# Order of transfers in one issue queue: earlier loads, earlier x transposes, hash halves apart, first casts on another engine

## Chip, cores, metric

The kernel runs on one core of a Trainium2 chip. The metric is the device time of one execution in microseconds (us). PE is the matmul engine, DVE the vector engine, ACT the scalar engine, POOL GpSimd. SP is the engine that issues most DMA transfers (161 of 180 in the trace of before): one queue, q1 of the profile, and its timeline shows them one after another in program order.

## The reference

Attention with hashed buckets, then a feed-forward layer. Inputs q, k, v are (4, 8, 768, 64): 32 heads of 768 tokens.

```
q_bits = (q @ proj > 0); k_bits = (k @ proj > 0)          # 6 bits each
mask   = bucket(q_bits) == bucket(k_bits)
attn   = softmax(where(mask, q @ k.T / 8, -1e9));  x = attn @ v
h = x @ w_in;  out = (h * cos(h)) @ w_out                 # 512 -> 2048 -> 512
```

## The kernel before

It works head by head. A *slot* is one head's turn and has nine *units*; in each unit PE makes 512 columns of scores, ACT takes their exponential, and PE multiplies the previous head's exponentials with v. In between stand small jobs, hung into a table `plan[(slot, unit)]`, so a job's place in the program is one pair of numbers:

- `load_pair(m)`: q, k, v of heads 2m and 2m+1, 1.18 MB in three transfers.
- `transpose` (PE) and `cast`: q and k of a head into the layout for the scores.
- the hash: PE multiplies with `proj` (one half for q, one for k), DVE compares with zero, and `place_bits` copies the bits by DMA into the rows beside the head's q and k. Heads are hashed in groups. Without its bits a head's scores can't start.
- `to_features(b, t)`: a DMA transpose of 128 tokens of batch b's attention output, six for a batch. The feed-forward layer ("MLP") of the batch needs them; the first MLP stands before slot 11.

All these transfers go through SP (w_in and w_out go through POOL), and SP waits at each transfer for what it depends on (in the trace of before up to 4.9 us at an x transpose, for DVE's `xtok`).

```python
def load_pair(m, heads=2):                       # three nc.sync.dma_start, buffer shared with pair m-3
    ...
def place_bits(heads, bits):
    for j, hd in enumerate(heads):
        for r in range(2):
            a = 32 * j + r * NBITS
            nc.sync.dma_start(out=e_all[D:KEXT, hd % NE, :, r * HB:(r + 1) * HB],
                              in_=bits[a:a + NBITS])
def to_features(b, t):
    nc.sync.dma_start_transpose(out=xT[:, :, b * S + t * P:b * S + (t + 1) * P],
                                in_=xtok[b][:, t, :])
# ... cut ...
def hash_at(slot, u, heads):
    # ... cut: first() and second() hash one half each; second() ends with place_bits ...
    at(slot, u, first)
    at(slot, u + 1, second)
TRANSPOSE = {2: (0, 0), 3: (0, 4), 4: (1, 4), 5: (2, 0), ...}        # cut
HASH = {(1, 0): [2, 3], (2, 6): [4, 5], (4, 5): [6, 7], (6, 6): [8, 9, 10, 11]}
# ... cut ...
for hd in range(12, NH, GH):
    hash_at(hd - 2, 5, list(range(hd, hd + GH)))
for m in range(3, NH // 2):
    at(max(0, 2 * m - 7), {3: 1, 4: 8}.get(m, 2), load_pair, m)
for b in range(B - 1):
    for t, (d, u) in enumerate(((1, 0), (1, 2), (1, 5), (1, 8), (2, 3), (2, 6))):
        at(H * (b + 1) + d, u, to_features, b, t)
# ... cut: in the prologue, head 0 is cast by DVE and ACT, head 1 is hashed ...
```

The softmax here doesn't subtract the row's maximum and nothing guards it: scores larger than these inputs give would overflow.

Of the kernel before, what the change touches and what calls it, by code (L numbers as in the profile page):

```python
# [10 lines left out]
BF16 = mybir.dt.bfloat16  # L11
# [11 lines left out]
def kernel(  # L23
# [19 lines left out]
    P = 128  # L43
# [5 lines left out]
    GH = 4  # L49
    VW = D + 1  # L50
    UNIT = 512
    HB = SB // 2 * P
    NU = SB * S // UNIT
# [8 lines left out]
    p_bits = ctx.enter_context(tc.tile_pool(name="p_bits", bufs=2))  # L62
# [14 lines left out]
    def load_pair(m, heads=2):  # L77
        b, h = divmod(2 * m, H)
        t = p_nat.tile([P, 2, 3, SB * D], FP32, name="nat")
        for i in range(0, 2, heads):  # L80
            for w, x in enumerate((q, k, v)):
                nc.sync.dma_start(
                    out=t[:, i:i + heads, w],
                    in_=x[b, h + i:h + i + heads].rearrange("h (p t) d -> p h (t d)", t=SB),
                )
            nat[2 * m + i] = t[:, i]
            nat[2 * m + i + heads - 1] = t[:, i + heads - 1]
# [48 lines left out]
    def cast(hd, r, engine="dve"):  # L136
        out_ap = e_all[0:D, hd % NE, :, r * HB:(r + 1) * HB]
        in_ap = f32[hd][r * D:(r + 1) * D]
        if engine == "act":
            nc.scalar.mul(out=out_ap, in_=in_ap, mul=QK_PRESCALE)  # L140
        else:
            nc.vector.tensor_scalar(
                out=out_ap, in0=in_ap, scalar1=QK_PRESCALE, scalar2=None, op0=ALU.mult,
            )

    def threshold(dst, src):
        nc.vector.tensor_scalar(  # L147
            out=dst, in0=src, scalar1=0.0, scalar2=0.5, op0=ALU.is_gt, op1=ALU.subtract,
        )


    def hash_group(heads, w, bits, pool=None, name="tp"):
        jp = (pool or ps_t).tile([P, 512], FP32, name=name, space=PSUM)
        for j, hd in enumerate(heads):
            nc.tensor.matmul(  # L155
                out=jp[32 * j:32 * (j + 1), 0:HB],
                lhsT=projx,
                rhs=f32[hd][:, w],
                start=True,
                stop=True,  # L160
            )
        n = 32 * len(heads)
        threshold(bits[0:n, w], jp[0:n, 0:HB])
# [5 lines that stand above are left out]
                nc.sync.dma_start(  # L169
                    out=e_all[D:KEXT, hd % NE, :, r * HB:(r + 1) * HB],  # L170
                    in_=bits[a:a + NBITS],
                )


    def hash_direct(hd, w):
        jp = ps_t.tile([P, 512], FP32, name="tp", space=PSUM)
        for r in range(2):
            nc.tensor.matmul(
                out=jp[32 * r:32 * r + NBITS, 0:HB],
                lhsT=projx[:, r * NBITS:(r + 1) * NBITS],  # L180
                rhs=f32[hd][:, w],
                start=True,
                stop=True,
            )
        for r in range(2):
            threshold(
                e_all[D:KEXT, hd % NE, w, r * HB:(r + 1) * HB],
                jp[32 * r:32 * r + NBITS, 0:HB],
            )
# [148 lines left out]
    for start, b in MLP_AT.items():  # L338
        for t in range(SB if b < B - 2 else SB - BRIDGE):
            f0 = 0  # L340
            for i, n in enumerate(RATE):
                slot, u = divmod(start * NU + t * len(RATE) + i, NU)
# [10 lines left out]
    def at(slot, u, f, *args):  # L353
        plan.setdefault((slot, u), []).append((f, args))


    def hash_at(slot, u, heads):
        bits = []
        first_bank = (ps_y, "y") if slot < min(MLP_AT) else (ps_t, "tp")

        def first():
            bits.append(p_bits.tile([P, 2, HB], BF16, name="bits"))
            hash_group(heads, 0, bits[0], *first_bank)

        def second():
            hash_group(heads, 1, bits[0])
            place_bits(heads, bits[0])

        at(slot, u, first)
        at(slot, u + 1, second)  # L370

    def both(slot, u, f, hd, step=1):
        at(slot, u, f, hd, 0)
        at(slot, u + step, f, hd, 1)


    TRANSPOSE = {2: (0, 0), 3: (0, 4), 4: (1, 4), 5: (2, 0), 6: (3, 0), 7: (3, 4),
                 8: (4, 2), 9: (5, 0), 10: (5, 4), 11: (6, 0), 12: (7, 0)}
    CAST = {1: (0, 2), 2: (0, 6), 3: (1, 2), 4: (2, 3), 5: (3, 2), 6: (4, 0), 7: (5, 2),
            8: (6, 3), 9: (7, 2), 10: (7, 5)}  # L380
    HASH = {(1, 0): [2, 3], (2, 6): [4, 5], (4, 5): [6, 7], (6, 6): [8, 9, 10, 11]}
    for hd in range(2, NH):
        slot, u = TRANSPOSE.get(hd, (hd - 5, 0))
        both(slot, u, transpose, hd, 2 if hd < 12 else 3)
    for hd in range(1, NH):
        both(*CAST.get(hd, (hd - 3, 1)), cast, hd)
    for (slot, u), heads in HASH.items():
        hash_at(slot, u, heads)
    for hd in range(12, NH, GH):
        hash_at(hd - 2, 5, list(range(hd, hd + GH)))  # L390
    for hd in range(2, NH):
        at(max(0, hd - 3) if hd != 3 else 1, 4 if hd != 4 else 7, cast_v, hd)
    for m in range(3, NH // 2):
        at(max(0, 2 * m - 7), {3: 1, 4: 8}.get(m, 2), load_pair, m)

    for b in range(B - 1):
        for t, (d, u) in enumerate(((1, 0), (1, 2), (1, 5), (1, 8), (2, 3), (2, 6))):
            at(H * (b + 1) + d, u, to_features, b, t)

    with tc.manual_schedule():  # L400
        warm = glob.tile([P, 1], BF16, name="warm")
        nc.vector.memset(warm, 0.0)
        nc.vector.memset(projx, 0.0)
        load_pair(0, 1)
        nc.scalar.dma_start(out=projx[0:D, 0:NBITS], in_=proj)
        nc.scalar.dma_start(out=projx[D:2 * D, NBITS:2 * NBITS], in_=proj)
        make_identity(nc, ident)
        once = glob.tile([P, 1], FP32, name="once")
        nc.scalar.activation(out=once, in_=warm, func=ACTF.Exp)
        load_pair(1)  # L410
        load_pair(2)
        nc.vector.memset(v_all[:, :, :, D:VW], 1.0)
        nc.vector.memset(delta, DELTA)
        for i in range(NE):
            (nc.vector if i < 3 else nc.gpsimd).memset(e_all[D:P, i], 0.0)
        wp = ps_y.tile([P, 512], FP32, name="y", space=PSUM)
        for _ in range(6):
            nc.tensor.matmul(  # L418
                out=wp[0:1], lhsT=warm, rhs=warm.to_broadcast([P, 512]), start=True, stop=True
            )  # L420
        transpose(0, 0, "act")
        transpose(0, 1)
        cast(0, 0)
        cast(0, 1, "act")
        hash_direct(0, 0)
        hash_direct(0, 1)
        transpose(1, 0, "act", ps_o, "o_att")
        transpose(1, 1, "act", ps_o, "o_att")
        bits = p_bits.tile([P, 2, HB], BF16, name="bits")
        for w in range(2):  # L430
            hash_group([1], w, bits)
        place_bits([1], bits)
        cast_v(0)
        cast_v(1)

        for hd in range(NH + 1):
            for i in WEIGHTS.get(hd, ()):
                load_weight(i)
            if hd in MLP_AT:
                for c in range(2):  # L440
                    hidden(MLP_AT[hd], c, wide)
            for u in range(NU):
                if hd < NH:
                    scores(hd, u)
                if hd > 0:
                    attend(hd - 1, u * NA, (u + 1) * NA)
                for b, t, f0, f1 in fill.get((hd, u), ()):
                    project(b, t, f0, f1)
                for f, args in plan.get((hd, u), ()):
                    f(*args)  # L450
                for b, t, f0, f1 in fill.get((hd, u), ()):
                    if f1 == NFF:
                        emit_out(b, t, "act")
            if hd > 0:
                normalize(hd - 1)
                if hd == NH:
                    for t in range(SB):
                        to_features(B - 1, t)

        ys = [(ps_y, "y"), (ps_t, "tp"), (ps_t, "tp")]  # L460
        for t in range(SB - BRIDGE, SB):
            project(B - 2, t, 0, NFF, *ys[t % 3])
            emit_out(B - 2, t, "act")
        for c in range(2):
            hidden(B - 1, c, wide)
        for t in range(SB):
            project(B - 1, t, 0, NFF, *ys[t % 3])
            emit_out(B - 1, t, "act", 2 if t == SB - 1 else 1)
# [30 lines left out]
```

## Time and profile before

| | before |
|---|---|
| time, median of the first 3 runs | 337.91 us (337.78 to 338.3) |
| span of the profiled run | 336.0 us |
| PE busy | 321.0 us, 96% |
| PE's waits for DMA, 10 to 100 us | xT 5.5, nat 2.5, bits 0.2 us |

The profiled run took 337.76 us.

From the page of the kernel before: each engine's busy time, and the granted PE clock in 40 slices of 8.4 us (tenths of full speed, 9 is 90% or more).

```profile
PE 321.0 (96%) x2794; PEld 193.5 (58%) x2794; DVE 177.9 (53%) x364; ACT 242.4 (72%) x453; POOL 83.2 (25%) x219
...
PEclk9999999799599999999999999999999999999999
```

Two slices have a low clock, the eighth (59 to 67 us) and the eleventh (84 to 92 us). The list of PE's waits between 10 and 100 us (line that waited, releaser, us in total, times, longest; `nat` is what `load_pair` fills, `ext` holds the operands of the scores with their bits, `xT` is what `to_features` fills):

```profile
PE st L284 <- DMA xT<-xtok: 5.5, 1, 5.5
PE tp L123 <- DMA nat<-in_q_dram: 2.5, 1, 2.5
...
PE st L201 <- DMA ext<-bits: 0.2, 1, 0.2
```

Two waits count: a transpose waiting for q of a later head, and the MLP waiting for a DMA transpose. The timeline of SP says why these came late (start, duration, what was issued, how many):

```profile
47.56 6.18 SPq L169 DMA_DIRECT2D ext<-bits  x8
53.86 0.37 SPq L82 DMA_DIRECT2D nat<-in_q_dram  x1
54.28 0.46 SPq L82 DMA_DIRECT2D nat<-in_k_dram  x1
54.78 0.47 SPq L82 DMA_DIRECT2D nat<-in_v_dram  x1
...
70.25 6.76 SPq L169 DMA_DIRECT2D ext<-bits  x8
77.06 1.23 SPq L253 DMA_TRANSPOSE xT<-xtok  x1
```

The eight bit transfers from 47.56 us are those of heads 8 to 11, 0.77 us each. Pair 7's load, the three lines from 53.86, stands behind them. The eight from 70.25 us are those of heads 12 to 15; the sixth x transpose, issued at 77.06, stands behind those. The table by stretches (length, PE busy, other engines, granted clock, DMA share, GB/s) shows what follows. The DMA share is the time of the packets that start in the stretch over that of 16 engines, so it can exceed 1.

```profile
core 0: us, PE busy (x) PEld busy (x) DVE busy (x) ACT busy (x) POOL busy (x), PEclk, DMA share, GB/s
56.80:59.30 2.50, 0.02 (x1) 0.00 (x0) 0.20 (x2) 0.77 (x2) 1.91 (x5) 1.00 1.00 320
60.20:63.50 3.30, 3.30 (x26) 2.27 (x24) 2.13 (x4) 2.46 (x5) 2.05 (x5) 0.50 1.28 153
...
80.80:86.30 5.50, 0.00 (x0) 0.03 (x1) 1.01 (x3) 0.49 (x1) 4.56 (x12) 0.79 1.27 185
86.30:90.90 4.60, 4.60 (x15) 2.22 (x16) 1.16 (x3) 1.47 (x3) 0.52 (x3) 0.51 1.16 270
90.90:98.80 7.90, 7.90 (x51) 4.74 (x49) 6.55 (x12) 5.73 (x12) 0.00 (x0) 1.00 0.28 62
```

In 56.8-59.3 and 80.8-86.3 PE does nothing. After each there is a stretch at half clock, 0.50 and 0.51; then full clock again. So in this trace each wait is paid twice. From 91 us on PE is busy to the end: there is nothing to gain there.

### The profile page before, as it was taken

How to read it: one execution, taken by the hardware profiler on the slowest of the kernel's cores; microseconds unless marked ns; L12 is line 12 of the kernel's file. 1: busy time of each engine (PE TensorE's matmuls, PEld its weight loads, DVE VectorE, ACT ScalarE, POOL GpSimd, SP SyncE). 2: the span in 40 equal slices, each digit the busy share in tenths (PEclk: the TensorE clock that was granted, in tenths of full speed). 3: DMA queues.
4: the chain of work that ended last, by engine and by line, in shares of the span. 5: the costliest groups of instructions: out<-in, count | busy, mean ns of one | idle time of the engine just before them, and what ended most of it. 6: DMA issues, size and time to landing. Idle time of an engine off the chain costs nothing.

```text
span 336.0 us, 7162 instructions
## 1 busy us (share of the span) xinstructions
PE 321.0 (96%) x2794; PEld 193.5 (58%) x2794; DVE 177.9 (53%) x364; ACT 242.4 (72%) x453; POOL 83.2 (25%) x219
## 2 busy tenths in 40 slices
PE   7999997996799999999999999999999999999995
PEld 3467665753366656665666656665665666565442
DVE  6878776556284445445884434444884011198100
ACT  4689888785279867878779867888779896477211
POOL 9974557316302223322002222422000000000000
PEclk9999999799599999999999999999999999999999
DMA  7856666939900400690600500650300011510021
GB/s 233 299 150 171 154 168 131 269 60 154 246 11 33 154 22 26 205 235 7 188 5 0 174 33 8 206 111 5 53 1 2 31 59 38 109 50 1 33 94 62
DMA packets 34398, 33.55 MB, mean 100 GB/s; under 512 B 15060, under 2 KB 30396, under 8 KB 34364
## 3 DMA queue, kind: packets, MB, share of 16 engines
q1 hardware_dynamic: 30732, 28.76, 30.0%
q0 software_dynamic: 3328, 4.20, 8.6%
q8 instruction: 22, 0.36, 0.5%
q10 hardware_dynamic: 304, 0.13, 0.1%
q14 instruction: 12, 0.10, 0.1%
HBM read 27.27 MB, written 6.29 MB: 100 GB/s over the span
## 4 chain that ended last, share of the span: by engine, by line
PE 88%; DMA 5%; ACT 3%; DVE 2%; SPq 1%; issue 0%; ACTq 0%; DVEq 0%
PE y L310 18%; PE st L201 17%; PE st L284 14%; PE o_att L230 10%; PE o_att L284 10%; PE tp L310 6%; PE tp L123 6%; PE tp L155 3%; DMA xT<-xtok 3%; ACT pt L209 2%; DMA nat<-in_q_dram 2%; PE o_att L220 1%; PE y L155 1%; DMA ext<-bits 1%; PE y L418 1%; DVE ext L147 1%
## 5 line engine op out<-in xcount | busy, mean ns | idle before, releaser
L209 ACT ACTIVATE pt<-st 128x512 f16<-128x512 f32 x288 | 157.1, 607 | 36.9 <-PE st L201 34.2
L201 PE MATMUL st<-ext 128*128 128x512 bf16 (+1 forms) x384 | 107.7, 328 | 0.9 <-ACT pt L209 0.5
L230 PEld LDWEIGHTS <-pt 128*128 128x128 f16 x1152 | 71.9, 98 | 37.0 <-issue 1.8
L310 PE MATMUL y<-wout,gt 128*128 128x512 f16 x288 | 88.1, 378 | 0.0
L230 PE MATMUL o_att<-v_ext,pt 128*128 128x65 f16 x1152 | 82.5, 195 | 0.0
L201 PEld LDWEIGHTS <-ext 128*128 128x128 bf16 x384 | 36.3, 98 | 25.3 <-issue 12.8
L107 POOL CAST v_ext<-nat 128x192 f16<-128x192 f32 x64 | 22.6, 383 | 114.0 <-PE o_att L230 113.9
L292 ACT ACTIVATE cs<-st 128x384 f16<-128x384 f32 x76 | 37.1, 490 | 17.0 <-PE st L284 16.7
L296 DVE TENSOR_TENSOR gt<-st,cs 128x384 f16<-128x384 f32 x76 | 41.9, 556 | 12.8 <-ACT cs L292 7.5
L310 PEld LDWEIGHTS <-gt 128*128 128x128 f16 x384 | 31.1, 98 | 14.9
L296 DVE TENSOR_TENSOR gt<-o_att,cs 128x384 f16<-128x384 f32 x52 | 28.9, 556 | 17.5 <-ACT cs L292 14.3
L244 DVE RECIPROCAL rec<-o_att 128x6 f32<-128x6 f32 x32 | 6.2, 194 | 55.8 <-PE o_att L230 55.7
L123 PE MATMUL tp<-ident,nat 128*128 128x128 f32 x186 | 32.1, 284 | 2.5 <-DMA nat<-in_q_dram 2.5
L292 ACT ACTIVATE cs<-o_att 128x384 f16<-128x384 f32 x52 | 25.5, 491 | 7.1 <-PE o_att L284 7.0
L284 PE MATMUL st<-xT,win_100 128*128 128x384 f16 x76 | 25.3, 333 | 5.5 <-DMA xT<-xtok 5.5
L123 PEld LDWEIGHTS tp<-ident,nat 128*128 128x128 f32 x186 | 22.9, 145 | 9.3 <-issue 3.8
L284 PE MATMUL st<-xT,win_101 128*128 128x384 f16 x76 | 25.4, 334 | 0.0
L284 PE MATMUL st<-xT,win_102 128*128 128x384 f16 x76 | 25.2, 332 | 0.0
L284 PE MATMUL st<-xT,win_103 128*128 128x384 f16 x76 | 25.2, 331 | 0.0
L310 PE MATMUL tp<-wout,gt 128*128 128x512 f16 x96 | 21.2, 379 | 0.0
L284 PEld LDWEIGHTS <-win_100 128*128 128x128 f16 x128 | 12.7, 99 | 14.2 <-issue 6.4
L111 POOL TENSOR_TENSOR vacc<-nat 128x192 f32<-128x192 f32 x32 | 19.5, 609 | 0.0
(207 smaller groups left out, 365.4 us busy)
## 6 DMA issues: line engine op xcount, KB each, us to landing
out_dram<-o_sb SPq DMA_DIRECT2D x23, 256.0 KB
nat<-in_q_dram SPq DMA_DIRECT2D x15, 384.0 KB
nat<-in_k_dram SPq DMA_DIRECT2D x15, 384.0 KB
nat<-in_v_dram SPq DMA_DIRECT2D x15, 384.0 KB
wout<-in_moe_w_out_dram POOLq DMA_DIRECT2D x8, 256.0 KB, 8.5
ext<-bits SPq DMA_DIRECT2D x62, 9.0 KB
win_100<-in_moe_w_in_dram POOLq DMA_DIRECT2D x2, 256.0 KB, 5.3
win_101<-in_moe_w_in_dram POOLq DMA_DIRECT2D x2, 256.0 KB, 5.1
```

The source lines that it names most:

```text
L107: nc.gpsimd.tensor_copy(out=dst[:, r], in_=src[:, r])
L111: nc.gpsimd.tensor_add(acc, x[:, 0:3 * D], x[:, 3 * D:6 * D])
L123: nc.tensor.matmul(out=tp[:, i * P:(i + 1) * P], lhsT=nat[hd][:, w, i * 2 * D:(i + 1) * 2 * D], rhs=ident, is_transpose=True, start=(i == ...
L155: nc.tensor.matmul(out=jp[32 * j:32 * (j + 1), 0:HB], lhsT=projx, rhs=f32[hd][:, w], start=True, stop=True,)
L201: nc.tensor.matmul(out=st[:, o:o + n], lhsT=e[:, 1, jt * P:(jt + 1) * P], rhs=e[:, 0, c:c + n], start=True, stop=True,)
L209: nc.scalar.activation(out=pts[hd][:, u * UNIT:(u + 1) * UNIT], in_=st, func=ACTF.Exp, bias=EXP_BIAS, scale=EXP_SCALE,)
L230: nc.tensor.matmul(out=o_ps[:, qt * VW:(qt + 1) * VW], lhsT=pts[hd][:, jt * S + qt * P:jt * S + (qt + 1) * P], rhs=v_all[:, hd % NV, jt], ...
L244: nc.vector.reciprocal(out=rec, in_=o_ps[:, :, D:VW])
L284: nc.tensor.matmul(out=hp[:, 0:TOK], lhsT=win_t[ft][:, ff * P:(ff + 1) * P], rhs=xT[:, ft, b * S + c * TOK:b * S + (c + 1) * TOK], start=( ...
L292: nc.scalar.activation(out=cs, in_=hp[:, 0:TOK], func=ACTF.Sin, bias=math.pi / 2.0, scale=1.0)
L296: nc.vector.tensor_tensor(out=gt, in0=hp[:, 0:TOK], in1=cs, op=ALU.mult)
L310: nc.tensor.matmul(out=y_state[b, t], lhsT=gates[b, c][ff][:, tt * P:(tt + 1) * P], rhs=wout_t[:, ff], start=(ff == 0), stop=(ff == NFF - 1),)
```

## The change

Its intent: loads one slot sooner and in front of the bit transfers, x transposes in front of the next bits, hash halves apart, first casts on ACT.

```diff
-    def hash_at(slot, u, heads):
+    def hash_at(slot, u, heads, step):
...
-        at(slot, u + 1, second)
+        at(slot, u + step, second)
...
-    TRANSPOSE = {2: (0, 0), 3: (0, 4), 4: (1, 4), 5: (2, 0), ...
+    TRANSPOSE = {2: (0, 0), 3: (0, 4), 4: (1, 3), 5: (1, 8), ...
-    HASH = {(1, 0): [2, 3], (2, 6): [4, 5], (4, 5): [6, 7], (6, 6): [8, 9, 10, 11]}
+    HASH = {(0, 0, 1): [1], (1, 0, 1): [2, 3], (2, 3, 2): [4, 5], (4, 4, 2): [6, 7],
+            (6, 5, 3): [8, 9, 10, 11]}
...
-        hash_at(hd - 2, 5, list(range(hd, hd + GH)))
+        hash_at(hd - 2, 5, list(range(hd, hd + GH)), 3)
...
-        at(max(0, 2 * m - 7), {3: 1, 4: 8}.get(m, 2), load_pair, m)
+        at(*{3: (0, 1), 4: (1, 5)}.get(m, (2 * m - 8, 5)), load_pair, m)
...
-        for t, (d, u) in enumerate(((1, 0), (1, 2), (1, 5), (1, 8), (2, 3), (2, 6))):
+        for t, (d, u) in enumerate(((1, 0), (1, 2), (1, 4), (1, 7), (2, 0), (2, 3))):
...
-        cast(0, 0)
         cast(0, 1, "act")
+        cast(0, 0, "act")
...
-        bits = p_bits.tile([P, 2, HB], BF16, name="bits")
-        for w in range(2):
-            hash_group([1], w, bits)
-        place_bits([1], bits)
```

(Cut: one cast moved by one unit, and the transposes of a head written out so that their second half may fall into the next slot.)

More of the change, by code (lines that the diff above doesn't have):

```diff
@@ L374, in both @@
         at(slot, u + step, f, hd, 1)
-    TRANSPOSE = {2: (0, 0), 3: (0, 4), 4: (1, 4), 5: (2, 0), 6: (3, 0), 7: (3, 4),
+    TRANSPOSE = {2: (0, 0), 3: (0, 4), 4: (1, 3), 5: (1, 8), 6: (3, 0), 7: (3, 4),
                  8: (4, 2), 9: (5, 0), 10: (5, 4), 11: (6, 0), 12: (7, 0)}
-    CAST = {1: (0, 2), 2: (0, 6), 3: (1, 2), 4: (2, 3), 5: (3, 2), 6: (4, 0), 7: (5, 2),
+    CAST = {1: (0, 2), 2: (0, 6), 3: (1, 2), 4: (2, 4), 5: (3, 2), 6: (4, 0), 7: (5, 2),
             8: (6, 3), 9: (7, 2), 10: (7, 5)}
-    HASH = {(1, 0): [2, 3], (2, 6): [4, 5], (4, 5): [6, 7], (6, 6): [8, 9, 10, 11]}
+    HASH = {(0, 0, 1): [1], (1, 0, 1): [2, 3], (2, 3, 2): [4, 5], (4, 4, 2): [6, 7],
+            (6, 5, 3): [8, 9, 10, 11]}
     for hd in range(2, NH):
         slot, u = TRANSPOSE.get(hd, (hd - 5, 0))
-        both(slot, u, transpose, hd, 2 if hd < 12 else 3)
+        at(slot, u, transpose, hd, 0)
+        at(*divmod(slot * NU + u + (2 if hd < 12 else 3), NU), transpose, hd, 1)
     for hd in range(1, NH):
         both(*CAST.get(hd, (hd - 3, 1)), cast, hd)
-    for (slot, u), heads in HASH.items():
-        hash_at(slot, u, heads)
+    for (slot, u, step), heads in HASH.items():
+        hash_at(slot, u, heads, step)
     for hd in range(12, NH, GH):
-        hash_at(hd - 2, 5, list(range(hd, hd + GH)))
+        hash_at(hd - 2, 5, list(range(hd, hd + GH)), 3)
     for hd in range(2, NH):
```

## The prediction

> **What bounds it.** PE is busy 321.0 of 336.0 us (profile, part 1), and after 91 us no PE wait is listed: only the first 91 us can give anything. There PE waits 5.5 us for xT<-xtok and 2.5 us for nat<-in_q_dram (list of waits). After each the granted clock falls: 0.66 in 60-65 us, 0.50 in 85-90 us (table by stretches).
>
> **Why.** SP issues transfers in program order, one hash-bit transfer every 0.77 us (timeline of SP).
> - Eight run from 47.56 to 53.7 us; the load of q/k/v pair 7 stands behind them, issued at 53.86, though its place is in slot 7, near 48. Head 14's transpose needs it in slot 9: PE stands until 59.34.
> - Eight more run from 70.25 to 77.0 us; the sixth x transpose stands behind them, issued at 77.06, among the w_out loads. The first MLP's second half needs it: PE stands from about 80.8 to 86.3 us.
>
> **Gains.**
> 1. Pair loads move six units forward, pair 7's ahead of the bits of heads 8-11. Its buffer is free once GpSimd has summed head 9 (44.5 us), so it is issued near 45 and lands near 51. Gone: 2.5 us, plus 1.2 us of slow clock (slot 9 took 8.3 us; without the wait 5.8; a warm slot 4.6).
> 2. All x transposes go out by slot 10 unit 3, ahead of the next bits. Gone: 5.5 us, plus 2.4 us of slow clock (16 matmuls from 86.30 to 91.28, against 2.6 us warm; chain of waits).
>
> [...]
>
> **Prologue.** A 1.28 us cast leaves DVE for ScalarE (0.84 us); head 1's hash leaves the prologue. First scores near 8.3 instead of 10.26 us. But head 1's bits go out near 11.7 instead of 10.94 us and packets follow 1.4-1.6 us later; slot 1 starts near 14.9 instead of 14.33. I expect 0 to 0.6 us lost.
>
> **Hash halves apart.** PE's work is the same (0.77 us per half); at most 0.3 us gained.
>
> **Costs.** Bits of heads 6-11 now stand behind 1.18 MB loads, which took 4.2 to 6.4 us. Head 8's would land near 52, when slot 8 starts; its wait was 0.2 us and may become 0.4-0.8. [...] pair 8's packets (issued 58.43) began at 62.3, after those of the transpose issued at 57.01. The x transposes likewise stand behind pair 8's load; I expect three by 66.5, MLP start near 67.
>
> **Sum.** -3.7 - 7.9 + 0.4 (prologue) + 0.5 (bits) - 0.1 = -10.8 us: 337.9 becomes 327.1, 3.2% faster. Range 325.0 to 331.2. Faster by over 2%: 0.88; within 2%: 0.11; slower: 0.01.
>
> **What would show it.** Right: no PE wait for nat or xT over 0.5 us; no slow-clock stretch after 10 us; first MLP matmul near 67 us; that MLP 20.9 us long; everything after parallel to before. Prologue: first scores near 8.3, slot 1 no earlier than before.
>
> **What would make it wrong.** Bits behind loads stop PE over 1 us at slots 6 or 8; w_out loads come late; x transposes behind pair 8's load delay the MLP's start; head 1's bits come early enough for the prologue to give its 2 us.

The sum: its 1.2 and 2.4 us of slow clock are read from the trace of before (at 86.30 us four matmuls took 1.44 us, against 0.65 at full clock). That trace has the packets of the transpose issued at 57.01 us from 59.76 to 63.57, and those of pair 8's load, issued at 58.43, from 62.26; that the x transposes would be held up by pair 8's load was the author's estimate, which e5_pair8 tests below.

## The result

| | before | after |
|---|---|---|
| time, median of 4 runs | 337.85 us (336.0 to 338.3) | 328.36 us (327.4 to 329.64) |
| span of the profiled run | 336.0 us | 325.6 us |

The ratio is 0.9732, 95% interval 0.9682 to 0.9781: faster. Ratios here are the mean time of one kernel's fast runs over that of the other's of the same rounds, so not quite the ratio of the medians quoted.

The same views of the kernel after. The page:

```profile
PE 317.8 (98%) x2794; PEld 191.9 (59%) x2794; DVE 177.0 (54%) x363; ACT 243.2 (75%) x454; POOL 82.4 (25%) x219
...
PEclk9999999999999999999999999999999999999999
```

No slice with a low clock is left. PE's waits from 10 to 100 us:

```profile
PE o_att L284 <- DMA xT<-xtok: 1.5, 1, 1.5
PE st L201 <- DMA ext<-bits: 0.8, 1, 0.8
```

The nat wait is gone. The one for xT is now at the MLP's start (line of its first bank, o_att), not in its middle, and 1.5 us long. SP's timeline:

```profile
44.37 0.37 SPq L82 DMA_DIRECT2D nat<-in_q_dram  x1
...
47.76 6.12 SPq L169 DMA_DIRECT2D ext<-bits  x8
...
57.32 10.93 SPq L253 DMA_TRANSPOSE xT<-xtok  x6
...
70.01 6.59 SPq L169 DMA_DIRECT2D ext<-bits  x8
```

Pair 7's load is issued at 44.37, in front of the bits of heads 8-11. The six x transposes begin at 57.32, and pair 9's load and the next bits come behind. The stretches:

```profile
56.80:59.30 2.50, 2.50 (x37) 1.90 (x35) 2.40 (x4) 2.50 (x6) 2.33 (x4) 1.00 0.97 283
60.20:63.50 3.30, 3.30 (x45) 2.51 (x46) 2.85 (x6) 3.30 (x8) 2.17 (x8) 1.00 1.56 168
66.10:67.50 1.40, 0.01 (x1) 0.10 (x2) 1.22 (x3) 1.24 (x1) 0.00 (x0) 1.00 1.34 254
67.50:77.90 10.40, 10.40 (x65) 6.26 (x65) 7.89 (x21) 7.32 (x15) 4.32 (x6) 1.00 1.00 227
77.90:88.10 10.20, 10.20 (x64) 6.16 (x63) 8.77 (x17) 7.64 (x17) 5.09 (x14) 1.00 0.74 119
```

The places where the kernel before stood or ran at half clock (first two lines) are now full at clock 1.00. The MLP's two halves take 10.4 and 10.2 us. PE stands only in 66.1-67.5.

Where the time came from, by the starts of slots in the two traces. A slot's start is here the first matmul of line 220, which opens each slot's output sum; the MLP's is its first matmul; its end is the start of the slot behind it.

| stretch | before, us | after, us | difference |
|---|---|---|---|
| to slot 1 | 14.54 | 14.77 | +0.2 |
| slots 1 to 8 (start of 1 to start of 8) | 37.44 | 36.85 | -0.6 |
| slot 8 | 4.38 | 4.41 | 0.0 |
| slot 9 (nat wait, half clock) | 8.31 | 4.41 | -3.9 |
| slot 10 to MLP start | 5.53 | 7.06 | +1.5 |
| MLP (xT wait, half clock) | 28.9 | 21.0 | -7.9 |
| from there to the end | 236.8 | 237.1 | +0.3 |

The sum is -10.4 us, the difference of the two spans. The medians differ by 9.5.

### The profile page after: what moved, and what is told of

Same layout as the page of the kernel before. It is cut to its first block, busy times and chain, and to the rows that moved or that the text cites. A ratio compares the mean times of both kernels' runs of the same rounds, so it can differ in the third digit from the quotient of the medians.

```text
span 325.6 us, 7156 instructions
## 1 busy us (share of the span) xinstructions
PE 317.8 (98%) x2794; PEld 191.9 (59%) x2794; DVE 177.0 (54%) x363; ACT 243.2 (75%) x454; POOL 82.4 (25%) x219
## 4 chain that ended last, share of the span: by engine, by line
PE 93%; DMA 3%; DVE 1%; SPq 1%; ACT 1%; issue 0%; ACTq 0%
PE y L310 19%; PE st L201 18%; PE st L284 15%; PE o_att L284 11%; PE o_att L230 10%; PE tp L310 6%; PE tp L123 6%; PE tp L155 3%; DMA xT<-xtok 2%; PE o_att L220 2%; PE y L155 1%; PE y L420 1%; SPq L253 1%; DMA ext<-bits 1%; DVE ext L147 1%; PE tp L178 0%
## 5 line engine op out<-in xcount | busy, mean ns | idle before, releaser
L201 PE MATMUL st<-ext 128*128 128x512 bf16 (+1 forms) x384 | 106.6, 326 | 1.5 <-DMA ext<-bits 0.8
L310 PE MATMUL y<-wout,gt 128*128 128x512 f16 x288 | 88.1, 378 | 0.0
L292 ACT ACTIVATE cs<-st 128x384 f16<-128x384 f32 x76 | 37.2, 490 | 11.0 <-PE st L284 10.9
L310 PEld LDWEIGHTS <-gt 128*128 128x128 f16 x384 | 31.1, 98 | 14.9
L296 DVE TENSOR_TENSOR gt<-o_att,cs 128x384 f16<-128x384 f32 x52 | 29.0, 557 | 15.6 <-ACT cs L292 11.7
L284 PE MATMUL st<-xT,win_100 128*128 128x384 f16 x76 | 24.8, 326 | 0.0
L284 PE MATMUL st<-xT,win_101 128*128 128x384 f16 x76 | 24.8, 326 | 0.0
L284 PE MATMUL st<-xT,win_102 128*128 128x384 f16 x76 | 24.8, 326 | 0.0
L284 PE MATMUL st<-xT,win_103 128*128 128x384 f16 x76 | 24.8, 326 | 0.0
L310 PE MATMUL tp<-wout,gt 128*128 128x512 f16 x96 | 21.2, 379 | 0.0
L284 PEld LDWEIGHTS <-win_100 128*128 128x128 f16 x128 | 12.5, 98 | 11.7 <-issue 3.0
```

Source lines behind the costliest of these rows:

```text
L201: nc.tensor.matmul(out=st[:, o:o + n], lhsT=e[:, 1, jt * P:(jt + 1) * P], rhs=e[:, 0, c:c + n], start=True, stop=True,)
L284: nc.tensor.matmul(out=hp[:, 0:TOK], lhsT=win_t[ft][:, ff * P:(ff + 1) * P], rhs=xT[:, ft, b * S + c * TOK:b * S + (c + 1) * TOK], start=( ...
L292: nc.scalar.activation(out=cs, in_=hp[:, 0:TOK], func=ACTF.Sin, bias=math.pi / 2.0, scale=1.0)
L296: nc.vector.tensor_tensor(out=gt, in0=hp[:, 0:TOK], in1=cs, op=ALU.mult)
L310: nc.tensor.matmul(out=y_state[b, t], lhsT=gates[b, c][ff][:, tt * P:(tt + 1) * P], rhs=wout_t[:, ff], start=(ff == 0), stop=(ff == NFF - 1),)
```

## The experiments

Theory: in the kernel before, two transfers stood behind sixteen bit transfers in SP's queue, and each of the two waits this caused was followed by a half-rate stretch of the PE clock. Rivals: DMA bandwidth, not order, made them late; the slow clock came of something else than standing; the prologue or the hash halves carry the gain.

All outputs are right. Medians and ranges in us; "before" is the kernel before in the same rounds on the same chip. Three chips were used, one for each block of four runs.

| run | this | before | ratio, 95% interval |
|---|---|---|---|
| e1_loads | 336.73 (334.39-341.18) | 336.95 (332.8-341.17) | 1.002 (0.995-1.010) |
| e2_xt | 331.17 (329.49-332.02) | same | 0.988 (0.982-0.994) |
| e3_rest | 332.48 (331.59-334.22) | same | 0.993 (0.987-0.998) |
| e4_warm | 335.81 (335.08-336.19) | same | 1.003 (0.995-1.011) |
| b_again | 336.85 (one run) | 336.9 (332.19-338.95) | none |
| h_only | 331.05 (330.73-331.56) | same | 0.982 (0.977-0.986) |
| e8_loads_hash | 335.44 (332.56-337.12) | same | 0.993 (0.985-1.001) |
| u1_hash | 333.25 (330.26-335.76) | same | 0.985 (0.978-0.992) |
| a_again | 328.1 (326.85-332.85) | 336.7 (332.56-338.55) | 0.981 (0.974-0.987) |
| e5_pair8 | 327.42 (326.64-330.06) | same | 0.981 (0.974-0.988) |
| e6_direct | 328.44 (327.89-328.94) | same | 0.982 (0.976-0.989) |
| e7_both | 326.73 (326.08-327.39) | same | 0.977 (0.971-0.983) |

The kernel before spreads far more on these chips than in its first runs, and the fast-run rule keeps only its quicker runs. That pulls the ratios up by half a per cent or more: a_again is the kernel after itself, and shows 0.981 where the first rounds showed 0.973. So I judge small effects by the traces. At the 2% of the verdicts, e1_loads, e2_xt, e3_rest and e8_loads_hash are "same" and the others "unclear" (b_again, a single run, has none): no part alone is shown faster by over 2%.

### e1_loads: the earlier loads alone

```diff
-        at(max(0, 2 * m - 7), {3: 1, 4: 8}.get(m, 2), load_pair, m)
+        at(*{3: (0, 1), 4: (1, 5)}.get(m, (2 * m - 8, 5)), load_pair, m)
```

> The kernel before with the earlier q/k/v loads alone. My theory (head 14's load stood behind eight hash-bit issues): the 2.5 us wait for nat in slot 9 and the slow clock of 60-65 us go, slot 10 starts 3.5 to 4 us earlier, the first MLP starts near 66.5 us; the wait for the sixth x transpose stays (5 to 7 us, it is still behind the bits), so 334.2 us, ratio 0.987 to 0.991. Rival (the DMA engines are short of bandwidth, the place in the queue does not matter): pair 7 still lands after 57 us and PE still waits over 1.5 us, ratio over 0.995.

Measured: ratio 1.002, nothing gained. The nat wait did go: slot 9 takes 4.41 us, as in the kernel after. But PE's list of waits has a new entry beside xT, twice, 5.0 us:

```profile
PE st L284 <- DMA xT<-xtok: 5.5, 1, 5.5
PE st L201 <- DMA ext<-bits: 5.0, 2, 3.4
```

The longest of the two is at slot 4. SP's timeline around it:

```profile
23.86 0.37 SPq L82 DMA_DIRECT2D nat<-in_q_dram  x1
...
27.21 3.07 SPq L169 DMA_DIRECT2D ext<-bits  x4
```

Pair 5's load (23.86 to 26.1) is now issued before the bits of heads 4 and 5 (27.21), and these land behind 1.18 MB. The stretches:

```profile
31.00:36.00 5.00, 1.59 (x24) 1.15 (x22) 2.80 (x7) 1.84 (x4) 2.85 (x9) 0.99 0.76 153
36.00:39.30 3.30, 3.30 (x26) 2.51 (x24) 0.56 (x1) 2.42 (x5) 0.00 (x0) 0.50 0.96 280
```

PE stands 3.4 us, and half clock follows: slots 3 and 4 take 15.6 us instead of 10.4 in the trace of before. The second new wait, 1.5 us, is at slot 8. So the loads alone trade one wait for two. In this trace head 4's second bit transfer had four of its six late increments by 32.1 us and the last two at 34.8 and 35.0, after the last packet of the loads before it (34.1), and PE went on at 35.1. A third of the bits' own packets, 16 of 48, also moved only from 33.9 us on. What held these up, no run isolates.

u1_hash below shows the same wait.

### e2_xt: the earlier x transposes alone

```diff
-        for t, (d, u) in enumerate(((1, 0), (1, 2), (1, 5), (1, 8), (2, 3), (2, 6))):
+        for t, (d, u) in enumerate(((1, 0), (1, 2), (1, 4), (1, 7), (2, 0), (2, 3))):
```

> The kernel before with the earlier x transposes alone. My theory: the 5.5 us wait in the middle of the first MLP goes together with the half-rate clock after it, 7.9 us in sum; the 2.5 us wait of slot 9 stays; 330.0 us, ratio 0.975 to 0.979. Rival (bandwidth: the w_out loads hold the transposes up wherever they are issued): a wait of 2 us or more is left in the MLP, and under half of the 7.9 us is gained.

Measured: 331.17 us, 5.8 us under before's median. In the trace no PE wait for xT is left and the MLP takes 21.0 us (72.0 to 93.0). The nat wait stays, 3.0 us, with half clock behind it (a mean of 0.66 in 60-65 us), and there is one for head 1's bits:

```profile
PE tp L123 <- DMA nat<-in_q_dram: 3.0, 1, 3.0
PE st L201 <- DMA ext<-bits: 1.4, 1, 1.4
```

The rival that the place in the queue doesn't matter falls: the w_out loads are the same, and the MLP doesn't wait. But the traffic is part of the cause. In the kernel before, the sixth x transpose was issued at 77.06 us with w_out loads under way and took 9.1 us to land; here it was issued at 70.21, before their first packet (77.44), and took 2.6. PE needed it at 80.8. With 2.6 us (an estimate from this trace) the one issued at 77.06 would have landed at 79.7. So by this estimate the bits did their harm by pushing it in among the w_out loads; no run takes those loads away. The ratio, 0.988, missed the expected 0.975 to 0.979, in part because before's quicker runs alone stand below it.

### e3_rest: the change without its loads and x transposes

```diff
-        at(*{3: (0, 1), 4: (1, 5)}.get(m, (2 * m - 8, 5)), load_pair, m)
+        at(max(0, 2 * m - 7), {3: 1, 4: 8}.get(m, 2), load_pair, m)
-        ... ((1, 0), (1, 2), (1, 4), (1, 7), (2, 0), (2, 3))
+        ... ((1, 0), (1, 2), (1, 5), (1, 8), (2, 3), (2, 6))
```

> The change without its earlier loads and without its earlier x transposes: prologue, casts, hash halves apart, first transposes only. My theory: scores start near 8.3 us, but slot 1 starts at 14.3 to 14.7, because head 1's bits go out later; both big waits stay; 337.5 to 338.3 us, ratio 0.998 to 1.002. Rival (the prologue's 2 us arrive at the end): 336 us or less, ratio under 0.995.

Measured: 332.48 us, 4.5 us under before's median. My expectation was wrong, and the prologue doesn't show as the reason: slot 1 starts at 15.81, later than in the trace of before (14.54). Single traces can't tell more here, for e2_xt, with the prologue of before, has 15.83. PE's waits for DMA are these two, and xT is not among them:

```profile
PE tp L123 <- DMA nat<-in_q_dram: 3.3, 1, 3.3
PE st L201 <- DMA ext<-bits: 1.6, 1, 1.6
```

The x transposes are where they were, and yet nothing waits for them. The reason stands in the part I had called worthless: with three units between the hash halves, the bits of heads 12 to 15 are issued in unit 8 of slot 10, behind the sixth x transpose in unit 6. Before, both were in unit 6, bits first.

### h_only: one number

```diff
-    def hash_at(slot, u, heads):
+    def hash_at(slot, u, heads, step=1):
-        at(slot, u + 1, second)
+        at(slot, u + step, second)
-        hash_at(hd - 2, 5, list(range(hd, hd + GH)))
+        hash_at(hd - 2, 5, list(range(hd, hd + GH)), 3)
```

> The kernel before with one number changed: the second hash half of the groups from head 12 on three units after the first instead of one, so that the bits of heads 12 to 15 are issued after the sixth x transpose; the x transposes stay where they were. My theory since e3_rest (it is the order of the two in SP's queue that counts, and either the x transposes or the bits may be moved): no wait for xT in the first MLP, which lasts 20.9 us instead of 28.9; the nat wait of slot 9 stays; about 330 us, ratio 0.975 to 0.983. Rival (e3_rest lost its xT wait through its later start, not through the order): the wait stays near 5 us, ratio over 0.995.

Measured: 331.05 us, ratio 0.982, 5.9 us under before's median. SP's timeline:

```profile
60.15 10.54 SPq L253 DMA_TRANSPOSE xT<-xtok  x5
71.40 6.73 SPq L169 DMA_DIRECT2D ext<-bits  x8
```

The transposes are issued before the bits, PE never waits for xT, and the MLP takes 21.0 us (70.8 to 91.8). That confirms the reading of e3_rest: it is the order of these two that counts, and the change reverses it twice, once from each side. Either part alone is enough for this gain.

### e8_loads_hash and u1_hash: what lets the loads gain

e8_loads_hash is before with the earlier loads and the new places of the first transposes and of the hash halves of heads 4 to 11:

```diff
-    HASH = {(1, 0): [2, 3], (2, 6): [4, 5], (4, 5): [6, 7], (6, 6): [8, 9, 10, 11]}
+    HASH = {(1, 0, 1): [2, 3], (2, 3, 2): [4, 5], (4, 4, 2): [6, 7], (6, 5, 3): [8, 9, 10, 11]}
     # and the load_pair and TRANSPOSE lines of the change
```

> The kernel before with the earlier loads and the new places of the first transposes and of the hash halves of heads 4 to 11; prologue, x transposes and later hash halves as before. My theory since e1_loads (the earlier loads put the bits of heads 4-5 and 8-9 behind 1.18 MB; the earlier first halves put them ahead again): no wait for bits over 1 us at slots 4 and 8, no wait for nat; slot 10 begins 3.5 to 4.2 us earlier than in the trace of before; the xT wait stays. About 334 us, ratio 0.985 to 0.992. Rival: the bits still wait 3 us or more at slot 4 or 8.

Measured: slot 10 starts at 60.51 us, 4.2 us before the 64.67 in the trace of before, and no wait for nat or bits is left. The whole gains little, because the xT waits grew: 6.0 us in the MLP's middle and 1.4 us at its start, the latter nearly the same as in the kernel after:

```profile
PE st L284 <- DMA xT<-xtok: 6.0, 1, 6.0
PE o_att L284 <- DMA xT<-xtok: 1.4, 1, 1.4
```

So about half of the loads' gain was given back: the span is 333.9 us against 336.0.

u1_hash is the kernel after with the hash halves of head 4 on put back:

```diff
-    HASH = {(0, 0, 1): [1], (1, 0, 1): [2, 3], (2, 3, 2): [4, 5], (4, 4, 2): [6, 7],
-            (6, 5, 3): [8, 9, 10, 11]}
+    HASH = {(0, 0, 1): [1], (1, 0, 1): [2, 3], (2, 6, 1): [4, 5], (4, 5, 1): [6, 7],
+            (6, 6, 1): [8, 9, 10, 11]}
-        hash_at(hd - 2, 5, list(range(hd, hd + GH)), 3)
+        hash_at(hd - 2, 5, list(range(hd, hd + GH)), 1)
```

> The kernel after with the hash halves of head 4 on back in their old places and one unit apart; loads, x transposes and prologue as after. My theory: the bits of heads 4-5 stand behind pair 5's load, so PE waits 3 to 4 us at slot 4 with a slow clock behind it, and 1 to 2 us at slot 8; the x transposes are still ahead of the next bits; 332 to 336 us, ratio 0.984 to 0.996 to before, so 4 to 7 us over after. Rival (halves apart only smooth ScalarE, as I predicted): within 1 us of after.

Measured: 333.25 us, about 5 over the kernel after (328.1 to 328.4 on other chips). PE stands 3.3 us for bits at slot 4, with half clock behind it (from 37.70 us three transposes took 0.69 us, from 39.65 on 0.36); slots 3 and 4 take 15.5 us. The expected wait at slot 8 did not come; the other one of the two is at slot 1.

```profile
PE st L201 <- DMA ext<-bits: 4.1, 2, 3.3
```

So the halves' new places are what keeps the bits of heads 4 and 5 ahead of pair 5's load. In the kernel after, the bits are issued at 25.83 and the load at 29.00:

```profile
25.83 3.06 SPq L169 DMA_DIRECT2D ext<-bits  x4
29.00 0.37 SPq L82 DMA_DIRECT2D nat<-in_q_dram  x1
```

### e4_warm: does standing cause the slow clock?

22 matmuls of no use fill the gap in the MLP of the kernel before.

```diff
+        if (b, c) == (0, 1):
+            keep = ps_y.tile([P, 512], FP32, name="y", space=PSUM)
+            for _ in range(22):
+                nc.tensor.matmul(out=keep, lhsT=delta, rhs=warm.to_broadcast([P, 512]), ...)
```

> The kernel before with 22 matmuls of no use (128x512, about 4.75 us at the full clock) set in front of the first MLP's second half, where PE stood 5.5 us for the sixth x transpose. My theory (the slow clock follows from PE standing): the real matmuls start at the same time as before, near 86.3 us, but at full rate; the granted clock stays at 1.0 in 80-95; the MLP ends 2.4 us earlier; 335.5 us, ratio 0.992 to 0.994. Rival (the clock falls for another reason, such as load or the DMA traffic): the clock still falls near 85-90, ratio 1.000 or more.

Measured, by stretches (the gap, and the second half of the MLP):

```profile
80.50:85.80 5.30, 4.89 (x22) 2.04 (x21) 1.12 (x3) 0.52 (x2) 4.26 (x11) 1.00 1.29 190
85.80:96.00 10.20, 10.16 (x63) 6.18 (x64) 7.58 (x14) 7.10 (x15) 0.83 (x4) 1.00 0.75 172
```

The 4.75 us for the 22 matmuls was an estimate from the trace of before, where two of 128x512 take 0.43 us at full clock (L310); they took 4.89. The real matmuls start at 85.84 us (86.30 before) and run at clock 1.00. The second half takes 10.2 us instead of 12.5 to its last matmul. The expected 2.4 us came as 2.2. The time doesn't decide: its ratio is 1.003, but before's runs in these rounds spread over 8 us. The trace does: with PE kept busy at the same DMA traffic (share 1.29 in the gap, 1.27 in the trace of before), the slow clock is gone there.

### b_again: before once more

Only a comment is added.

> The kernel before, unchanged but for a comment, for a second trace of it. I expect the same two waits (nat in slot 9, sixth x transpose in the first MLP), each followed by a slow clock; how long each is in this trace shows what part of the spread of this kernel's times (332.8 to 341.2 us on the last chip) is theirs. If the spread had another source, the two waits would be within 0.3 us of 2.5 and 5.5 us.

Measured: 336.85 us, and these waits:

```profile
PE st L284 <- DMA xT<-xtok: 4.0, 1, 4.0
PE tp L123 <- DMA nat<-in_q_dram: 2.6, 1, 2.6
PE o_att L284 <- DMA xT<-xtok: 1.5, 1, 1.5
```

The xT wait is split, 1.5 us at the MLP's start and 4.0 in its middle. Only one half-rate stretch follows, 3.41 us long, behind the 4.0 (clock 0.50 in 85.9-89.3); none behind the 2.6 us of nat (1.00 in 56-63). The first trace had two, of 3.41 and 6.83 us. So part of this kernel's spread is whether and how long the clock falls after a wait.

How much of it, the granted clocks tell. One stretch of 3.41 us at half clock lowers the mean clock of a run of some 335 us by 0.005. The 29 runs of before in these rounds lie on such steps. Of the fast ones, five have clock 1.000 and a median of 332.8 us, seven have 0.993 to 0.995 and 335.0, five have 0.990 and 336.6; those labelled slow have 0.990 to 0.980. So most of the spread goes with the number of half-rate stretches, up to four, and the rule for fast runs drops runs in which the change has most to gain. Two of the fast runs with one stretch are as slow as 337 us, so the clock is not all of it.

### a_again, e5_pair8, e6_direct, e7_both: what is left in the kernel after

a_again is the kernel after with a comment.

> The kernel after, unchanged but for a comment, as the measure for the three runs beside it and for a second trace. I expect 327.5 to 329.5 us, a wait of 1 to 2 us for xT at the start of the first MLP (the first x transpose stands behind pair 8's load), 0.3 to 1.5 us for head 1's bits, and none over 0.5 us besides.

Its waits are 0.8 us for xT at the MLP's start (I had expected 1 to 2) and 0.8 for head 1's bits.

e5_pair8 takes pair 8's load from in front of the x transposes and puts it behind them:

```diff
-        at(*{3: (0, 1), 4: (1, 5)}.get(m, (2 * m - 8, 5)), load_pair, m)
+        at(*{3: (0, 1), 4: (1, 5), 8: (10, 4)}.get(m, (2 * m - 8, 5)), load_pair, m)
```

> The kernel after with pair 8's load moved from slot 8 unit 5 behind the sixth x transpose (slot 10 unit 4); heads 16 and 17 need it only after the first MLP. My theory (the load's 1.18 MB stand ahead of the x transposes and cost the 1.5 us at the MLP's start): the first x transpose lands near 60 instead of 64 us, the wait at the MLP's start is under 0.3 us, 1.2 to 1.6 us less than the unchanged kernel beside it. Rival (the transposes are slow by themselves, 1.2 to 2.2 us of issue each): the wait stays over 1 us and the time is the same.

Measured: the first x transpose's packets end at 60.8 us instead of 65.1 (a_again), the third, which the MLP's start needs, has landed at 64.7 instead of 66.9, and PE has no wait for xT. Slot 10 to MLP start takes 5.5 us, against 6.3 in a_again and 7.1 in the first trace of after. The mechanism is as expected. The rival's issue times are those of the trace of after, 1.26 to 4.00 us for each of the six; here they are issued over 8.71 us instead of 10.93. In time, 327.42 against 328.1 us, the two can't be told apart.

e6_direct writes head 1's bits as head 0's, by DVE, without a transfer:

```diff
-    HASH = {(0, 0, 1): [1], (1, 0, 1): [2, 3], ...
+    both(0, 0, hash_direct, 1)
+    HASH = {(1, 0, 1): [2, 3], ...
```

> The kernel after with head 1's bits written by VectorE straight to their place, as head 0's are, instead of by a transfer: two more thresholds of 0.55 us, and no transfer of 2 us. My theory (the head 1 transfer eats the prologue's gain): no wait for bits at slot 1, which starts 0.4 to 0.9 us earlier than in the unchanged kernel beside it; the end likewise 0.3 to 0.9 us earlier. Rival (ScalarE's 0.51 us per unit binds slot 0 anyway, or VectorE does): slot 1 starts within 0.2 us of the unchanged one.

The figures in it are from the traces: a DVE threshold takes 0.55 us and seven of ACT's units 3.60 us (before), and PE waits for head 1's second bit transfer until 1.96 us after its issue at 12.45 (after).

Measured: slot 1 starts at 14.73 us, with the transfer at 14.71. My theory fell. The wait for bits is gone, but a wait for ACT stands in its place: PE can't start slot 1's scores before ACT has emptied a bank of slot 0's. The list of waits has 0.8 us for it, the longest of two, beside 1.8 us for xT, the wait that e5_pair8 removes. The edit has a cost of its own, two more DVE thresholds in slot 0, and its second exponential starts at 10.46 instead of 10.11 us in the trace of after; but just before it, at 9.7 us, PE also waited 0.4 us for nat, as it did not in the trace of after, so not all of this is the edit's. So it is open whether head 1's transfer alone, at no cost elsewhere, would give something.

e7_both has both edits.

> Both edits of the two runs before this one. If the waits are apart from one another, the gains add: 1.5 to 2.4 us less than the unchanged kernel after, near 326.5 us; if the earlier slot 1 only makes the x transposes wait longer, no more than the larger of the two.

Measured: 326.73 us, the lowest median and a narrow range, and no PE wait for xT or bits in its trace. Against a_again on the same chip it is 1.4 us less by medians, with ranges that overlap (326.08-327.39 and 326.85-332.85). It is at least as good as the kernel after; that it beats it is likely but not shown.

## Why the prediction was right, and where it was not

The total was right: 327.1 us foretold, 328.36 measured, inside the range; "faster by over 2%" had 0.88. By terms, with the trace of after:

- *"Gone: 2.5 us, plus 1.2 us of slow clock"* (slot 9, -3.7): measured -3.9. e1_loads, e8_loads_hash and the kernel after all have this slot at 4.41 us.
- *"Gone: 5.5 us, plus 2.4 us of slow clock"* (MLP, -7.9): measured -7.9. e4_warm shows that the slow part follows from standing: 2.2 us came back with the gap filled.
- *Prologue, +0.4*: first scores at 8.28 us (8.3 foretold), slot 1's first scores at 14.55 (14.9 foretold, 14.33 before), +0.2. This is less than traces differ by themselves: by the mark of the table above, slot 1 starts at 14.54 to 15.83 us in the seven traces with the prologue of before, and at 14.71 to 15.98 in the five with that of after. The reason that I gave, head 1's bits, is half of it: e6_direct shows that ACT's banks bind at the same moment.
- *Bits behind loads, +0.5 at slot 8*: did not come; no wait for bits at slots 4 to 8. This term was replaced by another that I had listed as a risk only: the x transposes behind pair 8's load, 1.5 us at the MLP's start. I put "three by 66.5, MLP start near 67"; PE was ready at 66.0 and started at 67.5. e5_pair8 shows the cause.
- *"Hash halves apart. PE's work is the same (0.77 us per half); at most 0.3 us gained"*: this is the step that failed. I costed the halves as work on PE and not as positions in SP's queue, although I knew that `place_bits` hangs on the second half. h_only shows that for heads 12 to 15 this part alone brings the MLP to 21.0 us, the same gain that I credited to the x transposes. u1_hash shows that for heads 4 and 5 it prevents a wait of 3.3 us and its slow clock, without which the earlier loads lose what they win (e1_loads: ratio 1.002).

The total survived because the two errors of attribution don't touch it: the gain for the MLP has two sufficient causes, both in the change, and the protection of the loads was in the change too. That they were there was luck as far as the prediction goes. So was the size: it took over the slow clock of one trace, three stretches of 3.41 us, without asking how often they come. The first four runs of before (336.0 to 338.3 us) were like that trace by their times; against the five runs with none of them (median 332.8, other chips) the 328.1 us of a_again are 1.4% less, not over 2%. Asked what the loads alone and the hash halves alone give, I would have said 3.7 and 0.3 us; by medians of before it was 0.2 us (e1_loads) and 5.9 us (h_only).

Open: what of the spread of the kernel before is not the slow clock; what the sixth x transpose would cost behind the bits but without the w_out loads; and whether the prologue has anything to give, for no run has it alone.

## What to carry to other kernels

When several kinds of transfer share one in-order queue, read a change of place as a change of order: write the queue down before and after, and ask for each transfer what now stands in front of it, small ones (0.77 us each, by eights) and large ones (1.18 MB) alike, and what traffic it then runs into (the sixth x transpose took 9.1 us among the w_out loads, 2.6 before them). Moving one transfer forward moves all the others back, so test parts alone before you credit one of them; here the largest gain had two sufficient causes and the second largest needed a partner. And count a PE wait of a few us with the slow clock that may follow it: here 1.2 us behind 2.5, and 2.4 behind 5.5.

## What the traces show of the clock and of issue

- Up to the end of the first MLP the half-rate stretches in the traces last 3.41 or 6.83 us. They followed waits of 2.5 us (before) and 1.6 us (e3_rest, clock 0.50 from 16.8 to 20.1 us), and did not follow waits of 2.6 us (b_again) and 1.5 us (after), so the length of the wait alone doesn't tell. In before the two stretches start at 60.13 and 84.02 us, seven times 3.41 us apart. Take windows of 3.41 us on such a grid in each trace, from 5 us to the end of the first MLP: PE was busy 0 to 37% of the window in front of each start of a half-rate stretch (26 and 5% in before), and 51% in one case (e3_rest, 13.3 to 16.7 us). Windows with 50% (e6_direct) or 55 to 59% (e1_loads, b_again, after, e2_xt, e8_loads_hash) had none behind them. The 2.6 us of b_again fell across two windows, busy 69 and 55%. This is a count over these traces; no run varies the share by itself.
- The first packet of a bit transfer came 1.40 us after the start of its issue (17.64 to 19.03 us, before) and 0.64 us after the end of it, for the issue itself took 0.76. SP took 0.77 us from one bit transfer to the next, and 1.19 to 3.46 us to issue a DMA transpose (median 1.26, before); six of them were issued over 10.9 us in the kernel after.
